# Weights and half of batch 1's x requested right behind batch 0's x; weights loaded row by row with columns picked by TensorE; transposes of x placed in other slots

## The chip, the core and the metric

The kernel runs on one core of a Trainium2 chip. The core has a matrix engine (TensorE, PE in the profile; PEld is its weight load), VectorE (DVE), ScalarE (ACT), GpSimd (POOL) and SyncE (SP), each with its own instruction stream, and sixteen DMA engines that move data between the chip's main memory (HBM), the on-chip memory SBUF and back. The metric is the device time of one execution in microseconds, lower is better.

## The reference

Two attention blocks through 32 inducing points, and behind them a gated feed-forward layer on every token. The shapes are B = 4 batches, N = 12416 tokens, m = 32 inducing points, C = 128 channels, 1536 hidden units.

```python
def mab(q, kv):
    s = scale * (q @ kv.transpose(0, 2, 1))
    s = s - s.max(-1, keepdims=True)
    a = np.exp(s)
    a /= a.sum(-1, keepdims=True) + 1e-09
    return a @ kv
h = mab(I, x)          # I: the inducing points, for each batch
y = mab(x, h)
...
gate = 1.0 / (1.0 + np.exp(-(y @ w_gate)))
val = y @ w_val
out = gate * val @ w_out
```

## The kernel before

The 12416 tokens of a batch lie as 128 partitions by 97 columns of tokens; the columns form six groups of 16 and one group of a single column. Each batch goes through three stages.

Stage 1 (`h`): x is loaded and converted to 16 bits (`x_load`, GpSimd's DMA queue, tile `xn`), turned so that channels lie on partitions (`xT`), scored against the inducing points (`s1_score`), turned into weights by an exponential (`s1_exp`, tile `a1T`), the weights are turned (tile `a1`, named `a` in the profile) and summed with x (`s1_sum`). For batch 0 TensorE turns x and the weights (`x_turn`, `s1_turn_pe`), since everything waits for it. For batches 1 to 3 DMA transposes on SyncE's queue do it (`x_transpose_dma`, L90, and `s1_turn_dma`, L251), beside the work of the batch before. The seven parts are combined (`plan_combine`), and `hw_fill` (L333) multiplies `h` with the gate and value weights, so that stage 3 needs `hw` alone: `hw` is laid out as six columns `i` of two halves `t`, each with 128 hidden units.

Stage 2 (each token's weights over the 32 points): `plan_stage2` scores a group, lowers by the maximum, takes the exponential, divides by the sum on GpSimd and turns the result by a DMA transpose (`s2_turn_dma`, L556, tile `a2r`). For batch 0 the first 4 columns are turned by TensorE, and the next 4 and 8 by the two transposes of L783 and L785.

Stage 3 is the main loop. It goes through blocks of 512 tokens and, within a block, through eight steps with two and one of the twelve hidden groups by turns. A step fills the value half (`hidden_mm`, L810) and, two steps ahead, the gate half, takes a tanh on ScalarE (L828), multiplies both on VectorE (`u`, L839), and TensorE projects `u` with `wo16` (L868). ScalarE scales the result, SyncE stores it (L888). From step 4 on, a product with two groups also waits for the gate fill of two steps later.

Nothing is scheduled by the compiler: each engine executes in the order in which the code is written. Two steps are one slot. The work of stages 1 and 2 is put into slots with `at(slot, ...)`, counted from the first slot `o` of a batch, and comes out between the products of that slot (`beside`). Engines don't wait for a slot, only for the semaphores that their instructions name; so SyncE and GpSimd run ahead of the slot as far as their data lets them. Loads from GpSimd take eight landing semaphores in turn, so the ninth request waits until the first load has landed, and so on.

Before the change the three weights are requested from within batch 0's stage 1 (L671, L674 and L707), the first half of batch 1's x behind the last of them (L716), the other three groups in slots 3, 14 and 17 (L922). The transposes of batch 1's x are in slots 0, 5, 10, 15, 20, 25 and 12 (L919). The last of the batch's seven parts is the single column, seventh in `groups`. Batch 1's first two groups are scored in slots 9 and 13 and summed from slots 16 and 18 on (L908).

Of the kernel before, what the change touches and what calls it, by code (L numbers as in the profile page):

```python
# [10 lines left out]
F16 = mybir.dt.float16  # L11
# [6 lines left out]
P = 128  # L18
# [7 lines left out]
def kernel(  # L26
# [9 lines left out]
    nc = tc.nc  # L36
    B, N, C = x.shape
    m = inducing.shape[0]
    F = moe_w_gate.shape[1]
    NJ = F // P  # L40
    NI = NJ // 2
    NCH = N // P
    NG = NCH // GC
# [8 lines left out]
    const = ctx.enter_context(tc.tile_pool(name="const", bufs=1))  # L52
# [20 lines left out]
    def x_load(b, s, first=0):  # L73
        c0, n = groups[s]
        if s == 0:
            c0, n = 0, n + NLO
        if b not in xn:
            xn[b] = xnp.tile([P, NCH, C], F16, tag="xn", name=f"xn_{b}")
        cuts = [c0, c0 + first, c0 + n] if first else [c0, c0 + n]
        for c, e in zip(cuts, cuts[1:]):  # L80
            nc.gpsimd.dma_start(xn[b][:, c:e, :], xv[b, :, c:e, :])  # L81
# [18 lines left out]
    def keep_on(n, tag):  # L100
        w_ps = ps.tile([P, 4, P], F32, tag=tag, name="w_ps")
        for _ in range(n):
            nc.tensor.matmul(w_ps[:], idle[:, 0, :], idle, start=True, stop=True)
# [18 lines left out]
    )  # L122
    x_load(0, 1)
    x_load(0, 2)
    wg16 = const.tile([P, NI, 2, P], F16, tag="wg16")
    wv16 = const.tile([P, NI, 2, P], F16, tag="wv16")
    wo16 = const.tile([P, NJ, C], F16, tag="wo16")
    x_load(0, 3)
    x_load(0, 4)
    x_load(0, 5, GC - BC)  # L130

    ident = const.tile([P, P], F16, tag="ident")
    nc.vector.tensor_copy(out=ident[:], in_=identf[:])
# [41 lines left out]
    def s1_sum(b, s, a1, tag):  # L175
        hp = ps.tile([P, C + 1], F32, tag=tag, name="hp_ps")
        s1_sum_pe(b, s, a1, hp, 0, 4)
        return s1_sum_keep(b, s, hp)
# [3 lines left out]
    def at(slot, make, late=False):  # L182
        plan.setdefault((slot, late), []).append(make)
# [34 lines left out]
    def s1_score(b, s, tag):  # L218
        s1 = s1_score_pe(b, s, tag)
        s1_max(b, s, s1)  # L220
        return s1
# [107 lines left out]
    def hw_fill(b, hf, tag):  # L329
        hw_ps = ps.tile([P, NI // 2, P], F32, tag=tag, name="hw_ps")  # L330
        for r in range(4):
            wsrc = wg16 if r < 2 else wv16
            nc.tensor.matmul(  # L333
                hw_ps[32 * r : 32 * r + 32, :, :],
                hT16[b][:],
                wsrc[:, ts(hf, NI // 2), r % 2, :],
                start=True,
                stop=True,
            )
        return hw_ps  # L340
# [292 lines left out]
    for p in range(-2, NS - 3):  # L633
        if p + 2 < NS - 1:
            x_turn(0, *groups[arrival[p + 2]], ("g2", "v2")[p % 2])
            if p < 0:
                keep_on((3, 2)[p + 2], "acc")
        if p + 1 >= 0:
            s = arrival[p + 1]
            a1T[s] = s1_exp(0, s, s1_score(0, s, ("g1", "v1")[(p + 1) % 2]))  # L640
        if p >= 0:
            s = arrival[p]
            a1[s] = s1_turn_copy(s, s1_turn_pe(0, s, a1T[s]))
        if p - 1 >= 0:
            s = arrival[p - 1]
            s1_sum(0, s, a1[s], "acc")
        if p + 1 == EARLY - 1:

            we = const.tile([P, EARLY], F32, tag="we")
            nc.vector.tensor_reduce(  # L650
                out=nml[:, 0:1], in_=nm1[:, 0:EARLY], axis=AX.X, op=ALU.min
            )
            nc.scalar.activation(
                out=we[:], in_=nm1[:, 0:EARLY], func=AF.Exp, bias=nml[:, 0:1], scale=-1.0
            )
            lw = const.tile([P, EARLY], F32, tag="lwe")
            nc.gpsimd.tensor_tensor(out=lw[:], in0=l1[:, 0:EARLY], in1=we[:], op=ALU.mult)
            add_tree(lw, EARLY, l1l[:, 0:1])
            hpart = [const.tile([P, C], F32, name=f"hpart{k}", tag=f"hpart{k}") for k in range(2)]

            def pool_part(p):
                nc.gpsimd.tensor_scalar_mul(
                    out=hpart[p > 0][:], in0=hst[:, p, 0:C], scalar1=we[:, p : p + 1]
                )
                if p > 0:
                    nc.gpsimd.tensor_tensor(
                        out=hpart[0][:], in0=hpart[0][:], in1=hpart[1][:], op=ALU.add
                    )

            pool_part(0)  # L670
            nc.gpsimd.dma_start(wg16[:], moe_w_gate.rearrange("c (i t f) -> c i t f", t=2, f=P))  # L671
        elif p == EARLY - 1:
            pool_part(1)
            nc.gpsimd.dma_start(wv16[:], moe_w_val.rearrange("c (i t f) -> c i t f", t=2, f=P))  # L674
        elif p == EARLY:
            pool_part(2)

# [26 lines left out]
    e32s = const.tile([P, m], F32, tag="e32s")  # L704
    nc.scalar.mul(out=e32s[:], in_=e32[:], mul=lsum[:])
    top = join_min(const, ml, (1, 3))
    nc.gpsimd.dma_start(wo16[:], moe_w_out.rearrange("(j p) c -> p j c", p=P))  # L707
    w4 = const.tile([P, 1], F32, tag="w4")
    nc.scalar.activation(out=w4[:], in_=ml[:], func=AF.Exp, bias=top[:], scale=-1.0)
    e32l = const.tile([P, m], F32, tag="e32l0")  # L710
# [2 lines left out]
    )  # L713
    e32w = const.tile([P, m], F32, tag="e32w")
    nc.scalar.mul(out=e32w[:], in_=e32[:], mul=w4[:])
    for g in range(3):  # L716
        x_load(1, g)

    a1[sc] = s1_turn_copy(sc, s1_turn_pe(0, sc, a1T[sc], "v2"))
    hps.append(s1_sum(0, sb, a1[sb], "m"))  # L720
# [173 lines left out]
    for b in range(B):  # L894
        o = base[b]
        more = b + 1 < B

        if b == 0:
            plan_stage2(0, groups[1][0], o, None, o + 3, soon=True)
            plan_stage2(0, groups[2][0], o + 5, o + 7, o + 18)  # L900
        for s in range(3 if b == 0 else 2, NG - 1):
            k = o + 16 * s - 28
            plan_stage2(b, groups[s][0], k, k + 2, k + (14 if more else 10))
        plan_stage2(b, groups[NG - 1][0], o + 56, o + 58, o + 66, far=o + 52)
        if not more:
            continue
        early = (
            [(9, (16, 17, 17)), (13, (18, 19, 19))]  # L908
            if b == 0
            else [(8, (15, 16, 17)), (12, (18, 19, 19))]  # L910
        )
        later = [(24, (31, 31, 31)), (28, (35, 35, 35)), (40, (47, 48, 49)), (44, (50, 51, 51))]
        for s, (score, total) in enumerate(early + later + [(32, (43, 43, 43))]):
            plan_stage1(b + 1, s, o + score, [o + e for e in total])
        plan_combine(b + 1, o + 52, o + 55, [(o + 72, o + 74), (o + 80, o + 82)])
        plan_stage2(b + 1, groups[0][0], o + 67, o + 70, o + 78)
        plan_stage2(b + 1, groups[1][0], o + 84, o + 86, o + 94)
        for g in range(NS):
            when = 3 * g if b else 5 * g if g < NG else 12  # L919
            at(o + when, lambda b=b, g=g: x_transpose_dma(b + 1, g))  # L920
            if b == 0 and 3 <= g < NG:
                at(o + (3, 14, 17)[g - 3], lambda g=g: x_load(1, g))  # L922
        if b + 2 < B:
            for g in range(NG):
                at(o + (24, 33, 42, 60, 60, 82)[g], lambda b=b, g=g: x_load(b + 2, g))

    def beside(slot, late):
        for make in plan.pop((slot, late), ()):
# [53 lines left out]
```

## Time and profile before

| | |
|---|---|
| median of the runs | 732.54 us |
| the three runs | 739.2, 731.61, 732.54 us |
| span of the profiled execution, first to last instruction | 731.7 us |
| mean granted clock of TensorE | 0.992 |
| VectorE busy | 706.5 us (97%) |
| ScalarE busy | 675.3 us (92%) |
| TensorE busy | 650.5 us (89%) |
| GpSimd busy | 420.0 us (57%) |
| moved by DMA | 65.21 MB, 89 GB/s in the mean |

The profile holds one execution; its times are counted from the start of its span. A row of a group gives line, engine, operation, tile written and tiles read, shape and count, then busy time and mean length, then the engine's idle time just before such instructions and what ended most of it. A row of the timeline gives start, length, the instruction, and in brackets the idle time before it with what ended it. The time of a DMA row is that from its issue to its landing. A busy share doesn't say what an engine is worth to the whole; the waits of the engine that is full nearly everywhere do.

### The profile page before, as it was taken

What the parts mean: (1) busy time and instruction counts of PE and PEld (TensorE: products, weight loads), DVE (VectorE), ACT (ScalarE), POOL (GpSimd) and SP (SyncE); (2) the same over time, 40 slices, a digit from 0 to 9 for tenths busy, and PEclk for the clock granted to TensorE, in tenths of its full rate; (3) what the DMA queues carried; (4) which work ended last, traced back from release to release, by engine and by line L of the source; (5) the groups of instructions that cost most, each with busy time, mean ns of one, the idle gap of its engine ahead of it and who ended that gap; (6) DMA issues with size and microseconds to landing.
All of it is one profiled execution on the core that took longest, in us unless ns stands there. A gap on an engine that the chain in (4) does not pass through costs nothing.

```text
span 731.7 us, 21494 instructions
## 1 busy us (share of the span) xinstructions
PE 650.5 (89%) x8437; PEld 391.8 (54%) x8437; DVE 706.5 (97%) x874; ACT 675.3 (92%) x1011; POOL 420.0 (57%) x702
## 2 busy tenths in 40 slices
PE   7978898999988989999988989899999899898887
PEld 3444555655555555555555555555555555555555
DVE  4879899999999999999999999999999999999998
ACT  4669899999999999999999999999999999999996
POOL 3534737588765457398747275487865665646200
PEclk9989999999999999999999999999999999999999
DMA  9899674235358363325188531321222222131311
GB/s 172 138 114 196 122 136 91 56 87 120 64 126 160 75 137 77 81 60 121 44 129 145 118 82 38 88 59 45 75 60 52 61 64 62 42 74 44 60 45 45
DMA packets 117750, 65.21 MB, mean 89 GB/s; under 512 B 101360, under 2 KB 102032, under 8 KB 117648
## 3 DMA queue, kind: packets, MB, share of 16 engines
q1 hardware_dynamic: 111936, 49.81, 31.7%
q0 software_dynamic: 5440, 13.90, 11.4%
q8 instruction: 66, 1.08, 0.6%
q14 instruction: 36, 0.29, 0.1%
q10 hardware_dynamic: 272, 0.13, 0.1%
HBM read 27.80 MB, written 25.43 MB: 73 GB/s over the span
## 4 chain that ended last, share of the span: by engine, by line
DVE 49%; issue 20%; PE 15%; ACT 10%; DMA 4%; DVEq 1%; POOL 0%; ACTq 0%; POOLq 0%
DVE u L839 47%; ACT t L828 9%; PE acc_ps L868 7%; PE v_ps L810 6%; DMA xn<-in_x_dram 2%; DVE nm L214 1%; DMA a2r<-a2n 1%; DMA a<-a1T 1%; DVEq L839 1%; PE hp_ps L262 1%; PE g_ps L810 1%; ACT a1T L227 0%; PE s_ps L202 0%; POOL xn L81 0%; PE xt_ps L624 0%
## 5 line engine op out<-in xcount | busy, mean ns | idle before, releaser
L839 DVE SCALAR_TENSOR_TENSOR u<-t,v_ps 128x1024 f16<-128x1024 f16 (+1 forms) x777 | 675.5, 945 | 8.4 <-PE g_ps L810 4.8
L828 ACT ACTIVATE t<-g_ps 128x1024 f16<-128x1024 f32 (+1 forms) x776 | 593.3, 818 | 36.2 <-ACT t L828 17.0
L810 PE MATMUL v_ps<-a2r,hwt 32*128 32x512 f16 (+1 forms) x1188 | 294.4, 372 | 65.3 <-DVE u L839 64.3
L868 PE MATMUL acc_ps<-wo,u 128*128 128x128 f16 x4656 | 329.4, 221 | 0.0
L868 PEld LDWEIGHTS <-u 128*128 128x128 f16 x4656 | 262.7, 98 | 89.1 <-issue 88.2
L810 PE MATMUL g_ps<-a2r,hwt 32*128 32x512 f16 (+1 forms) x1188 | 297.9, 379 | 2.9 <-DMA a2r<-a2n 2.9
L810 PEld LDWEIGHTS <-hwt 32*128 32x128 f16 x2400 | 90.7, 91 | 200.3 <-issue 152.9
L499 POOL TENSOR_TENSOR sum<-e 128x256 f32<-128x256 f16 (+1 forms) x23 | 15.5, 672 | 149.3 <-ACT e L491 142.7
L545 POOL TENSOR_TENSOR a2n<-e,rs 128x2048 f16<-128x2048 f16 (+2 forms) x24 | 86.2, 3594 | 8.3 <-DVE rs L517 6.6
L523 POOL TENSOR_TENSOR near<-sme,minus 128x16 f32<-128x16 f32 (+1 forms) x22 | 65.2, 2966 | 1.8
L886 ACT ACTIVATE o<-acc_ps 128x512 f32<-128x512 f32 x96 | 58.1, 605 | 0.3 <-PE acc_ps L868 0.3
L478 POOL TENSOR_SCALAR rise<-rise 128x256 f32<-128x256 f32 (+6 forms) x110 | 51.2, 466 | 9.7
L477 POOL TENSOR_TENSOR rise<-sc 128x256 f32<-128x256 f32 (+1 forms) x22 | 16.2, 738 | 38.7 <-ACT sc L467 38.5
L479 POOL TENSOR_TENSOR top<-top,rise 128x128 f32<-128x128 f32 (+3 forms) x88 | 28.4, 323 | 7.3
L499 POOL TENSOR_TENSOR sum<-sum 128x128 f32<-128x128 f32 (+3 forms) x92 | 28.5, 310 | 7.2
L477 POOL TENSOR_TENSOR rise<-top 128x128 f32<-128x128 f32 (+3 forms) x88 | 27.3, 310 | 6.9
L482 POOL TENSOR_TENSOR sc<-sc,top 128x512 f32<-128x512 f32 (+1 forms) x22 | 23.9, 1086 | 1.7
L430 PEld LDWEIGHTS <-xT 128*128 128x128 f16 x388 | 13.1, 96 | 12.0 <-issue 11.9
L430 PE MATMUL s_ps<-hT,xT 128*128 128x32 f16 x388 | 18.1, 178 | 0.1
L479 POOL TENSOR_TENSOR top<-sc,rise 128x256 f32<-128x256 f32 (+1 forms) x22 | 16.2, 738 | 1.8
L227 ACT ACTIVATE a1T<-s_ps,nm 128x512 f16<-128x512 f32 (+1 forms) x24 | 15.1, 629 | 1.7 <-DVE nm L214 1.7
L262 PE MATMUL hp_ps<-xn,a 128*32 128x128 f16 x388 | 14.1, 223 | 2.3 <-DMA a<-a1T 2.0
(121 smaller groups left out, 240.2 us busy)
## 6 DMA issues: line engine op xcount, KB each, us to landing
out_dram<-o SPq DMA_DIRECT2D x96, 256.0 KB, 2.2
xn<-in_x_dram POOLq DMA_DIRECT2D x19, 512.0 KB, 8.0
xn<-in_x_dram POOLq DMA_DIRECT2D x4, 544.0 KB, 5.7
a2r<-a2n SPq DMA_TRANSPOSE x29, 4.5
xn<-in_x_dram POOLq DMA_DIRECT2D x1, 384.0 KB, 15.1
wg<-in_moe_w_gate_dram POOLq DMA_DIRECT2D x1, 384.0 KB, 5.6
wv<-in_moe_w_val_dram POOLq DMA_DIRECT2D x1, 384.0 KB, 6.3
wo<-in_moe_w_out_dram POOLq DMA_DIRECT2D x1, 384.0 KB, 5.8
```

The costliest lines, as they stand in the source:

```text
L430: nc.tensor.matmul(s2[:, j, :], xT[b][:, c + j, :], hT16[b][:], start=(j == 0), stop=whole and j == j1 - 1, skip_group_check=True,)
L477: nc.gpsimd.tensor_tensor(out=r, in0=far, in1=near, op=ALU.subtract)
L478: nc.gpsimd.tensor_scalar_max(out=r, in0=r, scalar1=0.0)
L479: nc.gpsimd.tensor_tensor(out=top[:, 0:n, 0:w], in0=near, in1=r, op=ALU.add)
L499: nc.gpsimd.tensor_tensor(out=d[:, 0:n, :], in0=src[:, :, 0:w], in1=src[:, :, w : 2 * w], op=ALU.add)
L523: nc.gpsimd.tensor_tensor(out=near[:, 0:n], in0=sme[:, 0:n], in1=minus1[:, 0:n], op=ALU.pow)
L545: eng.tensor_tensor(out=a2n[:, 0:n, :, :], in0=e.unsqueeze(2).to_broadcast((P, n, 4, m)), in1=rs.unsqueeze(2).unsqueeze(3).to_broadcast((P ...
L810: st[what + "end"] = nc.tensor.matmul(pt[:, k, col : col + nb * P], hw[b][r : r + 32, j // 2, :], a2r[r : r + 32, o : o + nb, :].rearrange ...
L828: st["tanh"] = nc.scalar.activation(out=st["t"][:], in_=st["g"][:], func=AF.Tanh, scale=0.5)
L839: u = nc.vector.scalar_tensor_tensor(out=st["u"][:, :, c:e], in0=st["t"][:, :, c:e], scalar=1.0, in1=st["v"][:, :, c:e], op0=ALU.add, op1= ...
L868: nc.tensor.matmul(acc[0][(i // 2) % len(acc[0])][:, i, :], st["u"][:, k, ts(i, P)], wo16[:, j, :], start=(j == 0 and i in ((0, 2) if len( ...
L886: nc.scalar.mul(out=o32[:], in_=acc[0][0][:], mul=0.5)
```

## The change

The diff, with the parts left out that only move lines:

```diff
-    wg16 = const.tile([P, NI, 2, P], F16, tag="wg16")
-    wv16 = const.tile([P, NI, 2, P], F16, tag="wv16")
-    wo16 = const.tile([P, NJ, C], F16, tag="wo16")
     x_load(0, 3)
     x_load(0, 4)
     x_load(0, 5, GC - BC)
+    wg16 = const.tile([P, F], F16, tag="wg16")
+    wv16 = const.tile([P, F], F16, tag="wv16")
+    wo16 = const.tile([P, NJ, C], F16, tag="wo16")
+    nc.gpsimd.dma_start(wg16[:], moe_w_gate)
+    nc.gpsimd.dma_start(wv16[:], moe_w_val)
+    nc.gpsimd.dma_start(
+        wo16[:].rearrange("p j c -> p (j c)"), moe_w_out.rearrange("(p j) c -> p (j c)", j=NJ)
+    )
+    for g in range(3):
+        x_load(1, g)
...
-                wsrc[:, ts(hf, NI // 2), r % 2, :],
+                wsrc[:].rearrange("c (f i t) -> c i t f", i=NI, t=2)[:, ts(hf, NI // 2), r % 2, :],
...
-            nc.gpsimd.dma_start(wg16[:], moe_w_gate.rearrange("c (i t f) -> c i t f", t=2, f=P))
...
-            nc.gpsimd.dma_start(wv16[:], moe_w_val.rearrange("c (i t f) -> c i t f", t=2, f=P))
...
-    nc.gpsimd.dma_start(wo16[:], moe_w_out.rearrange("(j p) c -> p j c", p=P))
...
-    for g in range(3):
-        x_load(1, g)
...
-            [(9, (16, 17, 17)), (13, (18, 19, 19))]
+            [(11, (18, 19, 19)), (16, (23, 23, 23))]
             if b == 0
...
-            when = 3 * g if b else 5 * g if g < NG else 12
+            when = 3 * g if b else (7, 10, 13, 16, 19, 22, 11)[g]
             at(o + when, lambda b=b, g=g: x_transpose_dma(b + 1, g))
             if b == 0 and 3 <= g < NG:
-                at(o + (3, 14, 17)[g - 3], lambda g=g: x_load(1, g))
+                at(o + 2, lambda g=g: x_load(1, g))
         if b + 2 < B:
             for g in range(NG):
-                at(o + (24, 33, 42, 60, 60, 82)[g], lambda b=b, g=g: x_load(b + 2, g))
+                at(o + (28 if b == 0 else 24, 33, 42, 60, 60, 82)[g], lambda b=b, g=g: x_load(b + 2, g))
```

The hidden units are numbered anew: unit `f*12 + j` stands where `j*128 + f` stood. `wo` can then be loaded with whole rows, twelve of them to a partition, where it came in pieces of 128 numbers; the gate and value weights lie in SBUF as they lie in HBM, and the fills of `hw` pick every twelfth column.

GpSimd's stream at the program's start, before the change; `xn_92` is batch 0's x, `xn_496` batch 1's, and in brackets stand the semaphores waited for (`DMASW0` to `DMASW7` are landings of loads in turn):

```order
L81 DMA xn_92<-in_x_dram 128x2176
...
L81 DMA xn_92<-in_x_dram 128x512
L137 MEMSET ones_114 128x1
L139 MEMSET ones 128x128
L657 TENSOR_TENSOR lw<-l_0_132,we 128x3 [waits Activation_49]
...
L671 DMA wg_103<-in_moe_w_gate_dram 128x1536
...
L674 DMA wv_104<-in_moe_w_val_dram 128x1536 [waits DMASW0_49]
...
L707 DMA wo_105<-in_moe_w_out_dram 128x12x128 [waits DMASW1_49]
L81 DMA xn_496<-in_x_dram 128x2176 [waits DMASW2_49]
L81 DMA xn_496<-in_x_dram 128x2048 [waits DMASW3_49]
L81 DMA xn_496<-in_x_dram 128x2048 [waits DMASW4_49]
```

The same after it; `xn_113` is batch 1's x:

```order
L81 DMA xn_92<-in_x_dram 128x512
L131 DMA wg_107<-in_moe_w_gate_dram 128x1536
L132 DMA wv_108<-in_moe_w_val_dram 128x1536 [waits DMASW0_49]
L133 DMA wo_109<-in_moe_w_out_dram 128x1536 [waits DMASW1_49]
L81 DMA xn_113<-in_x_dram 128x2176 [waits DMASW2_49]
L81 DMA xn_113<-in_x_dram 128x2048 [waits DMASW3_49]
L81 DMA xn_113<-in_x_dram 128x2048 [waits DMASW4_49]
L144 MEMSET ones_121 128x1
L146 MEMSET ones 128x128
L664 TENSOR_TENSOR lw<-l_0_139,we 128x3 [waits Activation_49]
```

The six requests moved ahead of GpSimd's own first sums. The last of them waits for the landing of the fifth load of batch 0's x (`DMASW4`), and what follows it in the stream waits with it.

SyncE's stream from the first transposes of stage 2 to the second turned weights of batch 1, before; `xT_676` is the turned x of batch 1, `a_1089` and `a_1225` are its turned stage-1 weights:

```order
L556 DMA_TRANSPOSE a2r<-a2n 128x8x128 [waits Pool_49]
L90 DMA_TRANSPOSE xT_676<-xn_496 128x16x128 [waits DMASW2_49]
L888 DMA out_dram<-o_838 128x512 [waits Activation_49]
L90 DMA_TRANSPOSE xT_676<-xn_496 128x16x128 [waits DMASW3_49]
L556 DMA_TRANSPOSE a2r<-a2n 128x16x128 [waits Pool_49]
L888 DMA out_dram<-o_1006 128x512 [waits Activation_49]
L90 DMA_TRANSPOSE xT_676<-xn_496 128x16x128 [waits DMAHW0_49,DMASW4_49]
L251 DMA_TRANSPOSE a_1089<-a1T 128x4x128 [waits DMAHW1_49,PE_49,Activation_49]
L90 DMA_TRANSPOSE xT_676<-xn_496 128x1x128 [waits DMAHW2_49]
L888 DMA out_dram<-o_1142 128x512 [waits DMAHW3_49,Activation_49]
L251 DMA_TRANSPOSE a_1225<-a1T 128x4x128 [waits DMAHW4_49,PE_49,Activation_49]
```

And after; `xT_933`, `a_1154` and `a_1338` are the same three:

```order
L563 DMA_TRANSPOSE a2r<-a2n 128x8x128 [waits Pool_49]
L890 DMA out_dram<-o_838 128x512 [waits Activation_49]
L90 DMA_TRANSPOSE xT_933<-xn_113 128x16x128 [waits DMASW2_49]
L563 DMA_TRANSPOSE a2r<-a2n 128x16x128 [waits Pool_49]
L890 DMA out_dram<-o_1007 128x512 [waits Activation_49]
L90 DMA_TRANSPOSE xT_933<-xn_113 128x16x128 [waits DMASW3_49]
L90 DMA_TRANSPOSE xT_933<-xn_113 128x1x128 [waits DMAHW0_49]
L890 DMA out_dram<-o_1141 128x512 [waits DMAHW1_49,Activation_49]
L258 DMA_TRANSPOSE a_1154<-a1T 128x4x128 [waits DMAHW2_49,PE_49]
L90 DMA_TRANSPOSE xT_933<-xn_113 128x16x128 [waits DMAHW3_49,DMASW4_49]
L90 DMA_TRANSPOSE xT_933<-xn_113 128x16x128 [waits DMAHW4_49,DMASW5_49]
L890 DMA out_dram<-o_1275 128x512 [waits DMAHW5_49,Activation_49]
```

The first transpose of x moved behind the store of block 0, the second behind that of block 1, and the first turned weights of batch 1 behind that of block 2.

## The prediction

> **What bounds the kernel now.** I read the page's head and its costliest groups first, then busy time by stretches, then VectorE's timeline, then the chain of waits and the transfers. The groups show that the product of the two hidden halves on VectorE (L839) is the main load, and that its waiting for others is 8.4 us in all.
>
> ```profile
> span 731.7 us, 21494 instructions
> L839 DVE SCALAR_TENSOR_TENSOR u<-t,v_ps 128x1024 f16<-128x1024 f16 (+1 forms) x777 | 675.5, 945 | 8.4 <-PE g_ps L810 4.8
> ```
>
> The stretches (columns: window, length, busy time of PE, weight loads, VectorE, ScalarE, GpSimd, granted clock, DMA share, GB/s) say where. VectorE is full from 80 to 100 us, where only less VectorE work could help. It is not full from 37 to 46 us and from 60 to 80 us, where the granted clock falls too.
>
> ```profile
> 37.00:42.00 5.00, 1.71 (x19) 1.02 (x19) 2.04 (x3) 1.41 (x2) 0.82 (x2) 0.87 1.23 136
> 42.00:46.00 4.00, 4.00 (x25) 1.64 (x21) 2.13 (x3) 2.31 (x4) 1.29 (x3) 0.50 1.37 127
> 60.00:80.00 20.00, 16.85 (x247) 10.04 (x244) 16.93 (x21) 16.43 (x27) 7.83 (x17) 0.91 1.07 193
> 80.00:100.00 20.00, 17.47 (x246) 10.54 (x242) 20.00 (x25) 19.24 (x30) 13.78 (x23) 1.00 0.63 126
> ```
>
> VectorE's timeline (start, length, instruction, idle time before it) has the first product at 33.13 us and names six waits in two clusters: 3.42 + 1.41 + 0.38 = 5.21 us, and 1.45 + 0.62 + 1.00 = 3.07 us. Their 8.28 us are all but 0.1 of the 8.4, so nothing else is to be had there.
>
> ```profile
> 33.13 2.99 DVE L839 SCALAR_TENSOR_TENSOR u<-t,v_ps 128x1024 f16<-128x1024 f16 x3
> ...
> 42.46 1.82 DVE L839 SCALAR_TENSOR_TENSOR u<-t,v_ps 128x1024 f16<-128x1024 f16 x2 [3.42 <-PE v_ps L810]
> 45.69 1.82 DVE L839 SCALAR_TENSOR_TENSOR u<-t,v_ps 128x1024 f16<-128x1024 f16 x2 [1.41 <-PE g_ps L810]
> 47.88 2.95 DVE L839 SCALAR_TENSOR_TENSOR u<-t,v_ps 128x1024 f16<-128x1024 f16 x3 [0.38 <-PE g_ps L810]
> ...
> 74.32 0.69 DVE L839 SCALAR_TENSOR_TENSOR u<-t,v_ps 128x512 f16<-128x512 f16 x1 [1.45 <-PE g_ps L810]
> 75.63 1.82 DVE L839 SCALAR_TENSOR_TENSOR u<-t,v_ps 128x1024 f16<-128x1024 f16 x2 [0.62 <-PE g_ps L810]
> 78.45 8.13 DVE L839 SCALAR_TENSOR_TENSOR u<-t,v_ps 128x1024 f16<-128x1024 f16 x9 [1.00 <-PE g_ps L810]
> ```
>
> TensorE, which runs in order, was itself held by a transfer at the head of each cluster: by the turned weights of the second block (`a2r`), and by the turned stage-1 weights of batch 1 (`a`).
>
> ```profile
> 41.81 0.60 PE L810 MATMUL g_ps<-a2r,hwt 32*128 32x512 f16 x2 [2.92 <-DMA a2r<-a2n]
> 73.58 0.24 PE L262 MATMUL hp_ps<-xn,a 128*32 128x128 f16 x4 [1.97 <-DMA a<-a1T]
> ```
>
> The chain of waits agrees (start, length, what): the first part is set by a load of batch 0's x that landed at 18.0 us, and the transpose asked for at 33.18 us took 8.59.
>
> ```profile
> 4.00 14.04 DMA xn<-in_x_dram
> 33.18 8.59 DMA a2r<-a2n
> ```
>
> **The first cluster.** In the page's list of issues (the last number is the median time to landing) a transpose of 128x512 and one of 128x2048 take 2.6 and 4.5 us. What stood in the way of the one at 33.18 us were three loads of x, asked for from 26.94 us on; behind them here are the DMA rows of the first and the third, issued at 26.94 and 28.00 us.
>
> ```profile
> a<-a1T SPq DMA_TRANSPOSE x18, 2.6
> xT<-xn SPq DMA_TRANSPOSE x21, 4.5
> ```
> ```profile
> 26.94 1.62 POOL L81 DMA_DIRECT2D xn<-in_x_dram  x3
> ```
> ```profile
> xn<-in_x_dram POOLq DMA_DIRECT2D x1, 544.0 KB, 7.7
> xn<-in_x_dram POOLq DMA_DIRECT2D x1, 512.0 KB, 11.8
> ```
>
> The first landed at 34.6 us, the third at 39.8: 2.6 us for each 512 KB. The transpose landed 41.8 - 39.8 = 2.0 us after the last load, so it comes through once the loads are gone. After the change the three weights and these loads stand in GpSimd's queue right behind batch 0's x, of which 512 KB are still out at 18.0 us; it is in at 20.6. At 2.6 us per 512 KB, three weights of 384 KB take 5.9 us and 544 + 512 + 512 KB 8.0 us: the last load lands at 34.5 us, 5.3 us sooner, and the transpose at 36.5 us. TensorE began to wait at 41.81 - 2.92 = 38.9 us. With 2.4 us to spare the wait goes, and so do the two short ones behind it, which belong to the halved clock (0.50) after the idle time: 5.21 us. What is late next is the turned x, below.
>
> GpSimd pays with waits: each of the later requests waits for the landing of an earlier load, the last for the one that landed at 18.0 us. Behind it in GpSimd's order stand the sums of batch 0's first stage, which ran at 15.44 us.
>
> ```profile
> 15.44 0.19 POOL L657 TENSOR_TENSOR lw<-l,we 128x3 f32<-128x3 f32 x1 [9.58 <-ACT we L653]
> 21.69 0.60 POOL L662 TENSOR_SCALAR hpart<-hst,we 128x128 f32<-128x128 f32 x1 [2.29 <-ACT hst L277]
> ```
>
> From 15.44 to 21.69 us they spend 2.29 us on their last wait, so they have some slack, and two weight requests no longer stand among them. Starting at 19.0 us instead they need some 2.5 us and are at the piece of 21.69 us in time. I cost this at nothing; 1 us if x lands a microsecond later. The weights are in at 20.6 + 5.9 = 26.5 us, ahead of their first use at 28.39 us (below). That they come row by row, `wo` above all, saves packets beside work that waits for none of them: nothing.
>
> **The second cluster.** `a` was asked for at 66.53 us and reached TensorE at 73.58, 7.0 us instead of 2.6, beside two loads that GpSimd issued from 63.22 us on.
>
> ```profile
> 63.22 1.17 POOL L81 DMA_DIRECT2D xn<-in_x_dram  x2
> 66.53 1.31 SPq L251 DMA_TRANSPOSE a<-a1T  x1
> ```
>
> These loads move to slot 2, next to the one at 37.28 us. No load of x then stands before slot 28, and the stage-1 sum is planned five slots after its transpose instead of three; a slot, two products, is 8.13 / 9 x 2 = 1.8 us. So these 3.07 us go as well. TensorE and VectorE execute the same instructions, in other slots.
>
> **The weights' columns.** The fills of `hw` read their moving operand with a step of twelve elements instead of one. No row has such a step. The nearest are the same fills now, and a matmul whose moving operand has step zero:
>
> ```profile
> 28.39 0.34 PE L333 MATMUL hw_ps<-wg,hT 128*32 128x384 f16 x2
> ...
> 28.57 0.33 PE L333 MATMUL hw_ps<-wg,hT 128*32 128x384 f16 x2
> ...
> 29.67 0.32 PE L454 MATMUL s_ps<-hi,identb 128*128 128x384 bf16 x1 [0.23 <-POOL hi L445]
> ```
>
> 0.32 us against 0.33: the step need not cost anything, and a gain has no reason. If reading ran at a quarter, the two fills, 0.18 us apart, would add 3 x 2 x 0.18 = 1.1 us; the wait of 0.23 us at 29.67 takes up a part, so some 0.8 us would reach the start of the products. I take 0, nearest to the row of step zero. [...]
>
> **The turned x.** SyncE's transposes of batch 1's x now stand behind the store of block 0, issued at 48.11 us; 5.2 us sooner that is 42.9, and the first starts near 43.3. By then three loads are on their way (from 37.28 us; a lone load takes 5.2 us, two more 2.6 each: until 47.7 us). What a transpose costs beside a load differs. The first of these rows is the store; the DMA answers below it are, in order, of the transpose at 37.04, of the load at 37.28, of the load at 194.25, of the transpose at 195.28 and of a lone load at 161.5 us.
>
> ```profile
> 48.11 0.38 SPq L888 DMA_DIRECT2D out_dram<-o  x1
> ```
> ```profile
> 37.04 5.46 SPq L90 DMA_TRANSPOSE xT<-xn  x1
> ...
> 37.28 0.60 POOL L81 DMA_DIRECT2D xn<-in_x_dram  x1
> ```
> ```profile
> 194.25 0.65 POOL L81 DMA_DIRECT2D xn<-in_x_dram  x1
> ```
> ```profile
> 195.28 6.80 SPq L556 DMA_TRANSPOSE a2r<-a2n  x1
> ```
> ```profile
> xT<-xn SPq DMA_TRANSPOSE x1, 17.9
> ```
> ```profile
> xn<-in_x_dram POOLq DMA_DIRECT2D x1, 512.0 KB, 16.9
> ```
> ```profile
> xn<-in_x_dram POOLq DMA_DIRECT2D x1, 512.0 KB, 8.0
> ```
> ```profile
> a2r<-a2n SPq DMA_TRANSPOSE x1, 10.3
> ```
> ```profile
> xn<-in_x_dram POOLq DMA_DIRECT2D x1, 512.0 KB, 5.2
> ```
> ```profile
> 55.02 0.40 PE L202 MATMUL s_ps<-xT,indT 128*32 128x512 f16 x4 [0.17 <-DMA xT<-xn]
> ```
>
> A transpose asked for 0.24 us ahead of a load took 17.9 us; one asked for 1.0 us behind a load took 10.3, landing 3.3 us after that load, which took 8.0 instead of 5.2. Here the loads are six us ahead, nearest to the second pair: 47.7 + 3.3 = 51.0 us, or 53.8 if the loads stretch by 2.8 us as that one did. The scores (last row) need it two slots later than now: 55.0 - 5.2 + 3.6 = 53.4 us. That is a wait of 0 to 0.4 us, and up to 1.7 with the store's 256 KB in front (half of 2.6 us). I take 0.5. Behind it on SyncE stands the `a2r` of the second group: after an issue of 6.8 us as at 195.28 it starts at 50.1 us and lands 4.5 us later, while slot 15, which fills from it, is at 33.1 + 15 x 1.8 = 60.1 us.
>
> [...]
>
> **The sum.** 731.7 - 5.2 - 3.1 + 0.5 = 723.9 us of span. The runs shown are 731.61, 732.54 and 739.2 us, so the span is within 0.1 us of the lowest and 0.8 below the median; I add 0.4: 724.3 us.
>
> **The rivals.** *The turned x is late by some us*: the stretch (53.8) and the whole of the store (2.6) make it 56.4 us, 3.0 us of waiting, and a halved clock behind it another 1.41 + 0.38: 4.8 us, 731.7 - 8.3 + 4.8 + 0.4 = 728.6 us. For it speak the 7.0 us of `a`, against it the loads' lead. 0.20. *The loads still lie before the first transposes*, because GpSimd's waits let the queue run dry and the lead isn't had: only 3.1 us are gained, 729.0 us; it decides where the last load lands after 38.9 - 2.0 = 36.9 us. 0.07. [...] 0.09. *Slower*: transposes and loads throttle each other from the first turned x on, as at 37.04 us. At 43.3 us some 1.7 of the three loads are out; at 16.9 us each they need 28.7 us, x is turned 3.3 us later, at 75.3 us, and the wait is 21.9 + 1.8 us: 747.5 us. With 17.9 us for the transpose it is 61.2 us and 733.4. From a landing at 59.9 us on it eats the gain. For it stands that one pair of rows, against it the pair of 194 us. 0.09.
>
> **How the numbers follow.** The forecast holds 0.55, at 723.3 to 725.5 us. The range 722.8 to 729.5 takes in the two rivals near 729 and the slow reads; it leaves out the slower one and what is below the sum. One per cent, about what a measurement of this kernel can tell from no change, is 7.3 us: 725.2 and 739.9 us. Faster: most of the forecast (0.47) and half of the slow reads, 0.52. Slower: 0.06, the worse part of the last rival. Within: 0.42.
>
> **What would show it.** L839 with under 1.5 us of waiting; VectorE full in 37 to 46 and 60 to 80 us, with the clock at 1.00; the third load of batch 1 landed by 36.9 us; the first turned x before 53.4 us; the fill still at 0.33 us; the first product still at 33.1 us. The forecast is wrong if the products start over 0.5 us later, or if a new wait for `xT` or `a` stands before 80 us.

## The result and the profile after

The changed kernel takes 728.14 us (median of six runs, 727.66 to 728.62); the kernel before, beside it, 735.64 us (six runs, 731.61 to 739.2). The ratio is 0.9895, 95% interval 0.9855 to 0.9935: faster by 1.05%. The forecast was 724.3 us in a range of 722.8 to 729.5. The profiled execution took 727.66 us, of which 725.8 is its span.

The page and the groups of the kernel after (L841 is the product that was L839; lines behind the new loads have moved by two):

```profile
span 725.8 us, 21496 instructions
L841 DVE SCALAR_TENSOR_TENSOR u<-t,v_ps 128x1024 f16<-128x1024 f16 (+1 forms) x777 | 675.6, 944 | 3.1 <-PE g_ps L812 2.9
```

The product's waiting has gone from 8.4 to 3.1 us. The stretches (same columns as before: window, length, busy PE, weight loads, VectorE, ScalarE, GpSimd, clock, DMA share, GB/s) show VectorE nearly full where it was not, and a clock of 1.00 in place of 0.87, 0.50 and 0.91:

```profile
37.00:42.00 5.00, 4.46 (x61) 2.84 (x59) 4.70 (x7) 4.33 (x7) 2.75 (x7) 1.00 0.98 169
42.00:46.00 4.00, 3.69 (x55) 2.21 (x51) 4.00 (x7) 3.69 (x6) 1.44 (x4) 1.00 1.06 183
60.00:80.00 20.00, 17.51 (x277) 10.77 (x273) 19.53 (x24) 19.05 (x30) 10.92 (x13) 1.00 0.81 140
80.00:100.00 20.00, 17.98 (x278) 11.03 (x277) 19.98 (x26) 19.13 (x31) 8.61 (x21) 1.00 0.68 134
```

VectorE's timeline has two small waits where the clusters were, and two more, which the kernel before did not have, soon after batch 1 begins. Four like these stand at 336.89, 351.21, 508.31 and 522.62 us, the same places in batches 2 and 3.

```profile
32.26 1.82 DVE L841 SCALAR_TENSOR_TENSOR u<-t,v_ps 128x1024 f16<-128x1024 f16 x2
...
40.21 4.68 DVE L841 SCALAR_TENSOR_TENSOR u<-t,v_ps 128x1024 f16<-128x1024 f16 x5 [0.30 <-PE g_ps L812]
...
77.05 1.22 DVE L841 SCALAR_TENSOR_TENSOR u<-t,v_ps 128x1024 f16<-128x1024 f16 x1 [0.36 <-PE g_ps L812]
...
165.48 13.95 DVE L841 SCALAR_TENSOR_TENSOR u<-t,v_ps 128x1024 f16<-128x1024 f16 x16 [0.36 <-PE g_ps L812]
179.79 2.95 DVE L841 SCALAR_TENSOR_TENSOR u<-t,v_ps 128x1024 f16<-128x1024 f16 x3 [0.36 <-PE g_ps L812]
```

The rows of the fills of `hw` (L340, once L333) say what came in their place. One took 0.33 us before; the first of them in the timeline, and the group of all 16 for the gate weights (busy us, mean ns), now read:

```profile
27.53 0.86 PE L340 MATMUL hw_ps<-wg,hT 128*32 128x384 f16 x2
```
```profile
L340 PE MATMUL hw_ps<-wg,hT 128*32 128x384 f16 x16 | 6.5, 836 | 0.0
```

The transfers did what was asked of them. On GpSimd the last load of batch 1's first half is issued at 17.03 us, and the sums behind it run at 17.75 and 20.39 us:

```profile
17.03 0.53 POOL L81 DMA_DIRECT2D xn<-in_x_dram  x1 [1.93 <-DMA xn<-in_x_dram]
...
17.75 0.21 POOL L664 TENSOR_TENSOR lw<-l,we 128x3 f32<-128x3 f32 x1
...
20.39 0.60 POOL L669 TENSOR_SCALAR hpart<-hst,we 128x128 f32<-128x128 f32 x1 [0.16 <-POOL hpart L673]
```

In the lists of DMA issues (the last number is the time to landing) that load takes 16.1 us, so it lands at 33.1 us. The first transpose of `a2r`, asked for at 32.32 us, takes 2.6 instead of 8.6. The first turned x, issued on SyncE at 42.66 us, takes 9.0 and is there at 51.7 us.

```profile
xn<-in_x_dram POOLq DMA_DIRECT2D x1, 512.0 KB, 16.1
```
```profile
a2r<-a2n SPq DMA_TRANSPOSE x1, 2.6
```
```profile
xT<-xn SPq DMA_TRANSPOSE x1, 9.0
```

The books: 731.7 - 8.28 (both clusters) + 0.30 + 0.36 + 6 x 0.36 - 0.87 (the first product at 32.26 instead of 33.13 us) = 725.4 us, against 725.8 measured.

### The profile page after: what moved, and what is told of

It is laid out like the page before. It is cut to its first block, busy times and chain, and to the rows that moved or that the text cites. A ratio compares the mean times of both kernels' runs of the same rounds, so it can differ in the third digit from the quotient of the medians.

```text
span 725.8 us, 21496 instructions
## 1 busy us (share of the span) xinstructions
PE 648.4 (89%) x8437; PEld 390.4 (54%) x8437; DVE 706.7 (97%) x874; ACT 676.7 (93%) x1011; POOL 419.4 (58%) x702
## 4 chain that ended last, share of the span: by engine, by line
DVE 50%; issue 21%; PE 17%; ACT 9%; DMA 2%; DVEq 1%; POOL 0%; ACTq 0%; POOLq 0%
DVE u L841 47%; ACT t L830 8%; PE acc_ps L870 8%; PE v_ps L812 6%; DMA xn<-in_x_dram 2%; DVE nm L221 2%; PE hw_ps L340 1%; DVEq L841 1%; ACT a1T L234 1%; PE g_ps L812 0%; PE hp_ps L269 0%; POOL xn L81 0%; ACT hwt L419 0%; PE w_ps L103 0%; PE s_ps L437 0%
## 5 line engine op out<-in xcount | busy, mean ns | idle before, releaser
L841 DVE SCALAR_TENSOR_TENSOR u<-t,v_ps 128x1024 f16<-128x1024 f16 (+1 forms) x777 | 675.6, 944 | 3.1 <-PE g_ps L812 2.9
L81 POOL DMA_DIRECT2D xn<-in_x_dram x25 | 14.7, 596 | 6.6 <-DMA xn<-in_x_dram 5.7
```

The costliest lines, as they stand in the source:

```text
L841: u = nc.vector.scalar_tensor_tensor(out=st["u"][:, :, c:e], in0=st["t"][:, :, c:e], scalar=1.0, in1=st["v"][:, :, c:e], op0=ALU.add, op1= ...
```

## The experiments

Spans are compared, which lie 1.7 to 1.9 us under the times. The shortest of all are 722.9 to 723.1 us. All kernels but e2 number the hidden units as the kernel before does, if nothing else is said.

**The two halves of the change.** `e3_loads_early` has the early loads and batch 0's old slots; `e4_slots_only` has the kernel before's loads and the new slots.

```
e3:  the weights and x_load(1, 0..2) asked for behind batch 0's x, wo in its old pieces
     scores at (9, ..), (13, ..); x turned at 5 * g and 12; x_load(1, 3..5) at 3, 14, 17; x_load(2, 0) at 24
e4:  the reverse: loads where the kernel before has them,
     scores at (11, ..), (16, ..); x turned at 7, 10, 13, 16, 19, 22, 11; x_load(1, 3..5) at 2; x_load(2, 0) at 28
```

> The loads of the weights and of half of batch 1's x behind the first x, with the old numbering of the hidden units and every slot of batch 0 as before the change. My theory, that the first cluster is the three x loads running beside the first transpose and the second cluster is the load of batch 2's x beside a transpose, so that each falls to its own part of the change: the first cluster (3.42 + 1.41 + 0.38 = 5.2 us at 42 to 48 us) goes, the second (3.1 us at 74 to 79 us) stays; span 731.7 - 5.2 = 726.5 us, and 725.6 if the 0.9 us at the start come with the early loads too. Rival, the early loads do everything: span 722.5-723.7 us with no wait of the product over 1.5 us. Second rival, the old slots of x_load(1, 3..5) and of the turned x meet with the first transposes all the same: the first cluster stays at over 3 us and the span is 729-732 us.

> The kernel before with the moved slots alone (the scores of the first batch's next selection two to five steps later, the turned x, the loads of batch 1's second half and of batch 2's first block moved); weights and batch 1's first half are asked for where they were. My theory: the first cluster stays at 4 to 5.2 us or shifts by the two steps, at least half of it, because the three loads still land after 36.9 us beside the first transpose; the second goes; span 731.7 - 3.1 = 728.6 us, down to 726.5 if the later scores wait less. Rival, the later scores alone give the transposes the time that they need: both clusters go, span 723.4-724.5 us. Second rival, the loads of batch 1's second half, now asked for together, meet the first transposes: over 6 us of waits before 55 us and a span over 731 us.

Measured: e3 735.66 us median, ratio 0.9967 (0.9916 to 1.0017), its spans from 726.3 to 737.6 us, the longest that of the profiled execution; e4 729.42 us, ratio 0.9883 (0.9822 to 0.9944), spans 726.8 to 729.0 us. VectorE's timeline of e4 keeps the first cluster and has nothing of the second but one wait of 0.36 us:

```profile
41.15 1.82 DVE L839 SCALAR_TENSOR_TENSOR u<-t,v_ps 128x1024 f16<-128x1024 f16 x2 [2.65 <-PE v_ps L810]
43.55 1.82 DVE L839 SCALAR_TENSOR_TENSOR u<-t,v_ps 128x1024 f16<-128x1024 f16 x2 [0.59 <-PE g_ps L810]
45.72 2.95 DVE L839 SCALAR_TENSOR_TENSOR u<-t,v_ps 128x1024 f16<-128x1024 f16 x3 [0.35 <-PE g_ps L810]
```

e3 has the opposite. Its profiled execution is one of its longer ones, so only the order of events is read from it. VectorE is full where the first cluster stood; from 60 to 80 us it waits, at a clock of 0.70, behind a transpose of `a` that was asked for at 61.35 us beside two loads of x and took 7.2 us:

```profile
42.00:46.00 4.00, 3.75 (x56) 2.38 (x56) 4.00 (x7) 3.90 (x6) 1.27 (x6) 1.00 1.00 184
46.00:50.00 4.00, 3.49 (x46) 1.97 (x41) 4.00 (x6) 3.80 (x7) 4.00 (x2) 1.00 0.67 122
...
60.00:80.00 20.00, 17.65 (x226) 10.73 (x224) 13.85 (x17) 13.66 (x22) 8.36 (x11) 0.70 0.84 139
```

Behind it stands, in this execution, a third stall of which the profile before has nothing: 5.07 us and, right behind, 1.20 and 0.69. There a transpose of `a` asked for at 91.27 us, beside two loads issued from 90.64 us on, took 10.8 us.

```profile
103.47 0.69 DVE L839 SCALAR_TENSOR_TENSOR u<-t,v_ps 128x512 f16<-128x512 f16 x1 [5.07 <-PE g_ps L810]
```

So in these profiles each cluster belongs to its own half, as the theory had it, but e3 as a whole missed the expected 726.5 us: the early loads alone can't be told from no change, and which of the old slots makes the third stall, and whether the shorter runs have it, is open. What the theory had wrong is that a cluster has one size. The first is 5.2 us before and 3.6 in e4. e2 (further down), with loads and slots at their old places, has 1.27 + 1.41 us there, then 1.63 + 1.20 + 0.54 from 54 us on, where the scores wait for the turned x, and 2.93 + 1.20 + 0.85 in the second cluster. The slots are therefore worth more than 3.1 us: e4's ratio is 8.6 us of some 735. They also take away spread: over 7 us in the runs of the kernel before, 2.2 us in e4, 1.0 in the changed kernel.

**Which of the moved slots.** Each of these undoes one of the moves in `e1_old_columns` (further down), whose spans are 723.0 to 723.7 us, with one of 725.4.

```
e9:   at(o + 2, ...)                           ->  at(o + (3, 14, 17)[g - 3], ...)     x_load(1, 3..5)
e10:  (7, 10, 13, 16, 19, 22, 11)[g]           ->  5 * g if g < NG else 12            the turned x
e8:   [(11, (18, 19, 19)), (16, (23, 23, 23))] ->  [(9, (16, 17, 17)), (13, (18, 19, 19))]
e7:   28 if b == 0 else 24                     ->  24                                 x_load(2, 0)
```

> As e1_old_columns, but the second half of batch 1's x is asked for at slots 3, 14 and 17 again instead of all at slot 2. Theory, that the second cluster and the long spans come from loads of x that meet a transpose of a or of x at 58 to 72 us, and that the halved clock behind each stall makes them longer: new waits of the product between 60 and 80 us, 3 us or more in the profiled run, with the granted clock under 1.00 there; spans spread over 3 us or more, from 724 us up, median 2 to 10 us above that of e1_old_columns. Rival, the later scores of the first batch's end (slots 11 and 16) already give the transposes time: no wait over 0.5 us after 50 us and a median within 1 us of e1_old_columns (724-726 us).

> As e1_old_columns, but batch 1's x is turned at slots 0, 5, 10, 15, 20, 25 and 12 again, so that the first transpose is asked for within 1.5 us of the three loads of x at slot 2. The rival of the prediction that ends slower, transposes and loads throttling each other from the first on: the first transpose takes 15 us or more instead of 9, the loads 10 to 17 us each, a2r of the second group comes late behind it on SyncE, TensorE stalls over 2 us before 60 us, and the span is 726-733 us. Theory of this run, that the transpose's slack covers it since the scores come at slot 11: the transpose and the loads take long, but no wait of the product over 0.5 us, span 722.5-724.5 us.

> As e1_old_columns, but the scores of batch 1's first two blocks stand at slots 9 and 13 again and their sums at 16, 17 and 18, 19, while the transposes of x and the loads stay where the change put them. Theory, that the later scores are needed because the first turned x lands at 51.7 us now: at slot 9 the scores want it at 33 + 9 x 1.8 = 49.5 us, so TensorE waits 1.5 to 3 us there, the clock halves behind it, and the span is 725-728 us. Rival, the scores have slack: no wait over 0.5 us, span 722.5-723.7 us.

> As e1_old_columns, but the first load of batch 2's x stands at slot 24 again instead of 28. Theory, that this move is the smallest part: the load is asked for some 7 us sooner, at 77 to 83 us, where the transposes of batch 1 are still under way; no wait over 0.5 us, span within 0.5 us of e1_old_columns (722.5-724.2 us). Rival, as in the run with the early loads alone, where loads at 90.6 us met a transpose of a asked for at 91.3 us and TensorE waited 5 us: a stall of 2 us or more between 75 and 105 us with the clock at 0.5 behind it, span 726 us or more in at least half of the runs.

Measured, medians and ratios: e9 728.29 us, 0.9895 (0.986 to 0.9931); e10 724.91, 0.9858 (0.9795 to 0.992); e8 729.41, 0.9909 (0.9879 to 0.9939); e7 725.17, 0.9855 (0.9794 to 0.9916). Spans: e9 724.0 to 728.8, e10 722.9 to 725.3, e8 725.8 to 729.3, e7 722.9 to 724.1.

In e9 a part of the second cluster is back, with its cause. The profiled execution is one of its two best, with 0.73 + 0.36 us of waits at a clock of 1.00, less than the 3 us expected; the other eight runs are 2 to 4.8 us longer, with mean clocks of 0.991 to 0.998, and no trace shows where they lose it. The transpose of `a`, asked for at 57.47 us, took 9.6 us beside two loads issued from 57.24 us on, where the changed kernel's took 4.0, and TensorE waited for it:

```profile
67.11 0.24 PE L267 MATMUL hp_ps<-xn,a 128*32 128x128 f16 x4 [1.26 <-DMA a<-a1T]
```
```profile
67.86 0.69 DVE L839 SCALAR_TENSOR_TENSOR u<-t,v_ps 128x512 f16<-128x512 f16 x1 [0.73 <-PE g_ps L810]
68.91 8.86 DVE L839 SCALAR_TENSOR_TENSOR u<-t,v_ps 128x1024 f16<-128x1024 f16 x10 [0.36 <-PE g_ps L810]
```
```profile
a<-a1T SPq DMA_TRANSPOSE x1, 9.6
```

In e10 the meeting that the prediction's slower rival was made of does take place: a turned x asked for at 35.32 us, 1.1 us ahead of three loads, takes 15.1 us. It does no harm: it is there at 50.4 us, sooner than the changed kernel's 51.7, and with the scores at slot 11 nothing needs it before 52.30 us.

```profile
35.32 10.50 SPq L90 DMA_TRANSPOSE xT<-xn  x1
```
```profile
xT<-xn SPq DMA_TRANSPOSE x1, 15.1
```

In e8 the scores want the turned x before it lands at 52.2 us: TensorE stands still from 49.8 us on, VectorE waits 1.87 us, and 1.20 + 0.54 more once TensorE has begun again. The stretches show the clock at 0.50 from 52 to 58 us:

```profile
52.26 0.62 PE L207 MATMUL s_ps<-xT,indT 128*32 128x512 f16 x4 [2.48 <-DMA xT<-xn]
```
```profile
52.92 0.69 DVE L219 TENSOR_REDUCE nm<-s_ps 128x1 f32<-128x512 f32 x1 [1.87 <-PE s_ps L207]
55.41 1.82 DVE L839 SCALAR_TENSOR_TENSOR u<-t,v_ps 128x1024 f16<-128x1024 f16 x2 [1.20 <-PE g_ps L810]
57.77 4.67 DVE L839 SCALAR_TENSOR_TENSOR u<-t,v_ps 128x1024 f16<-128x1024 f16 x5 [0.54 <-PE g_ps L810]
```
```profile
51.00:52.00 1.00, 0.00 (x0) 0.00 (x0) 0.05 (x1) 0.12 (x1) 0.92 (x2) 0.83 1.28 113
52.00:53.00 1.00, 0.74 (x6) 0.21 (x5) 0.08 (x1) 0.00 (x0) 0.83 (x3) 0.50 1.25 284
...
57.00:58.00 1.00, 1.00 (x8) 0.22 (x6) 0.46 (x2) 0.72 (x2) 0.92 (x2) 0.50 0.01 1
58.00:59.00 1.00, 1.00 (x14) 0.86 (x12) 1.00 (x2) 1.00 (x2) 0.18 (x1) 0.75 0.21 43
```

So two moves work, the loads at slot 2 and the later scores; the turned x and batch 2's first load could have stayed where they were. Whether the later scores are still needed with the transposes back at their old slots was not run.

**What the halved clock costs by itself.** `e11_keep_busy` is e8 with work for TensorE during its wait.

```
+        if b == 1 and s == 0:
+            for k in range(11):
+                nc.tensor.matmul(s1[0:32, :], indT[:], wo16[:, 0:4, :]..., start=True, stop=True)
```

> As e8_scores_back, where TensorE stands still from 49.8 to 52.3 us for the turned x, the clock then is 0.5 from 51.2 to 58.5 us, and VectorE waits 1.87 + 1.20 + 0.54 us; here 11 matmuls of 128x512 whose result nobody uses (the scores overwrite it) are put on TensorE ahead of that wait, 11 x 0.22 = 2.4 us at full clock. Theory, that the two later waits are the price of the halved clock and not of the stall itself: the clock stays at 1.00 from 50 to 60 us in the profile, the first wait stays at 1.5 to 2.2 us, the two behind it shrink to under 0.5 us together, the span is 725.5-726.0 us, and the median lies 1 to 3 us under the 729.4 us of e8_scores_back. Rival, they come from TensorE having lost its lead over VectorE: the clock stays at 1.00 or nearly, but over 1.2 us of waits still follow the first, span 727 us or more. Second rival, matmuls that use 32 columns of the array don't keep the clock up: it halves all the same and nothing changes, or the fillers cost 2 us more.

Measured: 729.17 us median (727.64 to 731.79), span of the profiled execution 726.1 against 727.2 in e8. In the profile the clock stays at 1.00 and the two waits behind the first are gone, though the turned x came 0.7 us later (53.0 us) and the first wait is longer:

```profile
53.45 0.69 DVE L224 TENSOR_REDUCE nm<-s_ps 128x1 f32<-128x512 f32 x1 [2.41 <-PE s_ps L212]
```
```profile
50.00:60.00 10.00, 8.69 (x87) 4.75 (x85) 7.45 (x9) 6.73 (x11) 6.91 (x16) 1.00 0.97 171
```

In these two profiles that tells the halved clock from the lost lead: the later waits were the clock's, 1.7 us of them. The medians do not differ as expected. Four of e11's ten runs have a mean clock of 1.000 and spans of 725.8 to 726.4 us, none of e8's ten has; in the other six it is 0.992 to 0.998, so there it fell all the same, and no trace shows where.

**The columns.** `e1_old_columns` is the changed kernel with contiguous columns, `e2_new_columns` the kernel before with the new ones; `e5_step2` and `e6_step6` number the units so that TensorE reads every second or sixth element, 4 or 12 bytes from one to the next.

```
e1:  wsrc[:].rearrange("c (i t f) -> c i t f", i=NI, t=2)      wo16 <- "(j p) c -> p j c"
e2:  the kernel before with wg16, wv16 as [P, F], wo "(p j) c -> p (j c)" and "c (f i t) -> c i t f"
e5:  "c (i f t) -> c i t f"                                    wo in 6 pieces of 2 rows
e6:  "c (h f i t) -> c h i t f", h=2                           wo in 2 pieces of 6 rows
```

> The changed kernel with the hidden units numbered as before: the weights are still asked for behind the first x and every slot stays moved, but TensorE reads 128 contiguous elements of a weight row instead of every twelfth. My theory, that the six waits of 0.36 us at the fills of batches 1 to 3 and the fill at 831 ns come from the reads 24 bytes apart: the fill falls back to 326 to 337 ns, the six waits (6 x 0.36 = 2.2 us) go, the eight fills at the start take 0.5 us instead of 1.5, and the span falls from 725.8 to 722.5-723.7 us. Rival, the moved slots make these waits: the fill is short again, but the waits of the product at 165 to 523 us stay, and the span is 724.8-725.8 us. Second rival, the output weights in 128 x 12 pieces of 256 bytes take the software queue longer than one block: batch 1's first x lands more than 2 us later than at 28.8 us, and 1 to 3 us come back before 50 us.

> The kernel before with the new numbering of the hidden units alone: the weights are loaded row by row at their old places, the columns picked by TensorE 24 bytes apart, no slot moved. My theory: the fill goes from 335 to 831 ns, six new waits of about 0.36 us appear at the fills of batches 1 to 3, the first product comes 0.5 to 1 us later, both clusters of waits (5.2 us at 42 to 48 us, 3.1 us at 74 to 79 us) stay; span 731.7 + 2.2 + 0.5 to 1.0 = 734.4-734.9 us, which is slower than the kernel before. Rival, the fills hide behind TensorE's idle time and the small waits belong to the moved slots: no such waits, span 731.7-732.5 us. Second rival, loading in whole rows is what removed the clusters: the span falls below 730 us.

> As e1_old_columns, but the units are numbered so that TensorE reads every second element of a weight row: 4 bytes from one to the next, four of them in 16 bytes. [...] Rival, any step but one costs: fill at 500 to 831 ns and six waits of about 0.36 us.

> [...] Rival, by elements as soon as they lie some bytes apart: 831 ns and six waits of 0.36 us. [...]

Measured: e1 725.21 us, ratio 0.983 (0.9769 to 0.9891), spans 723.0 to 723.7 us in three of four runs; e2 735.42 us, 0.9961 (0.9918 to 1.0004); one run each of e5 and e6, with spans of 723.1 and 725.7 us (in e6 the first product comes 0.8 us later than in e5, for a reason that isn't the reads', see below). The groups of the fill in e1, e2, e5 and e6, in that order:

```profile
L338 PE MATMUL hw_ps<-wg,hT 128*32 128x384 f16 x16 | 2.5, 335 | 0.0
```
```profile
L333 PE MATMUL hw_ps<-wg,hT 128*32 128x384 f16 x16 | 6.6, 840 | 0.0
```
```profile
L338 PE MATMUL hw_ps<-wg,hT 128*32 128x384 f16 x16 | 2.6, 341 | 0.0
```
```profile
L338 PE MATMUL hw_ps<-wg,hT 128*32 128x384 f16 x16 | 5.2, 668 | 0.0
```

The stretch from 140 to 700 us holds nothing else that differs, and VectorE's third number in it is the price. First e1, then the changed kernel, e2 and e6:

```profile
140.00:700.00 560.00, 505.34 (x6507) 305.18 (x6506) 559.97 (x662) 538.81 (x794) 343.32 (x558) 1.00 0.37 81
```
```profile
140.00:700.00 560.00, 505.19 (x6472) 304.23 (x6471) 557.78 (x658) 537.40 (x791) 341.85 (x557) 1.00 0.36 80
```
```profile
140.00:700.00 560.00, 505.62 (x6482) 304.72 (x6479) 557.77 (x660) 537.12 (x793) 350.49 (x573) 1.00 0.36 80
```
```profile
140.00:700.00 560.00, 505.58 (x6486) 304.99 (x6485) 558.67 (x659) 537.78 (x792) 342.79 (x558) 1.00 0.36 80
```

559.97 - 557.78 = 2.2 us, six waits of 0.36, with the new slots and with the old ones: the reads make these waits, not the slots. At 12 bytes it is 559.97 - 558.67 = 1.3 us, in six waits of 0.20 to 0.23; at 4 bytes nothing (559.97 again). The rivals of the two runs, 500 to 831 ns at 4 bytes and 831 at 12, did not come true with 341 and 668. The two small waits of 0.30 and 0.36 us at 40 and 77 us stand in e1 and e5 too, so they are not the reads'. The first is in every profile with the early loads; the second is in every one with the later scores, e4 among them, and not in e8 and e11, which have the scores back. That e2 would be slower than the kernel before was not seen: both vary by more than 2 us in their clusters. Nor did the output weights in small pieces delay batch 1's x: in e1 its first load lands at 28.6 us, against 28.8 in the changed kernel.

**The parts that are needed, alone.** `e12_needed_only` is e1 with the moves of e10 and e7 undone together.

> The parts that the runs so far show to be needed, and no other: the early loads with the old numbering of the hidden units, the second half of batch 1's x at slot 2, the later scores; batch 1's turned x and batch 2's first load stand where they stood before the change. Theory, that the moved turns and the moved load of batch 2 bring nothing: span 722.5-724.2 us in all runs but those in which the fifth load of x lands at 18 us (725.4 us), median 724.5-725.5 us, ratio to the kernel before 0.980 to 0.988. Rival, the two moves guard against a meeting of loads and transposes that the single undoings did not show because the other was still in place: spans over 726 us in a third of the runs or more.

Measured: 724.88 us median (724.84 to 725.71, six runs), ratio 0.9866 (0.9821 to 0.9911), spans 723.0 to 723.8 us. In these runs the two moves guard against nothing. Its median is 3.3 us under the changed kernel's; by the ratios to the kernel before beside each it is 2.1 us.

## Why the prediction came out as it did

The forecast was the likeliest case and the right one: both clusters went, for the causes it named. It was 3.8 us too low: 3.7 from two terms, the columns and what lies around the span, less 0.7 from three smaller ones, and 0.8 between the sum of these (at the end of this section) and the median.

**First cluster, 5.2 us: right.** The third load landed at 33.1 us (forecast 34.5, deciding point 36.9), the transpose took 2.6 us, and e4, which has the loads late, keeps 2.65 + 0.59 + 0.35 us, so this size too is that of one execution. The view that the short waits belong to the halved clock is what e11 shows for another stall.

**Second cluster, 3.1 us: right cause, one sample.** The loads at slot 2 take it away, and e9, without them, waits 1.26 us for `a` again. But 3.07 us is what it cost in one execution; the kernel before loses other amounts in others, and the mean clock roughly goes with them: 728.9 us of span at 0.995, 733.9 at 0.990, 739.7 at 0.986 among the runs that stood beside the first four experiments. A forecast against the profiled time is sound, one against a median of three such runs is not.

**The turned x, 0.5 us: nothing, in time by 0.7 us.** It landed at 51.7 us, in the forecast's 51.0 to 53.8; the scores began at 52.33 us instead of 53.4, in the main because this execution ran 0.9 us ahead (see below). It took 9.0 us, twice the median of 4.5 us in the profile before; others took 15.1 us (e10) and 17.9 (before), and what makes those so long stays open. The cover named, scores two slots later, is real: without it e8 loses 1.87 + 1.20 + 0.54 = 3.6 us, between the 1.7 us of the main case and the 4.8 us of the rival "late by some us".

**GpSimd's waits at nothing: right.** The sums ran at 17.75 us (forecast 19.0), the piece of 21.69 us at 20.39.

**The columns at 0: wrong, and this is the step that failed.** "I take 0, nearest to the row of step zero": step zero reads one element again and again and says nothing of a read that goes on to another address each time. Measured, the fill took 836 ns at 24 bytes from one element to the next, 668 at 12, 341 at 4 and 335 at 2. No run had shown such a read when the slow reads got their chance of 0.09, and the quarter of the rate behind their 0.8 us is shown by none since: 836 for 335 ns is 2.5 times. They were also priced at the wrong place. At the start, where the 0.8 us were to fall, the fills do take 1.0 us longer (27.53 to 29.06 us, against 28.39 to 28.90 before), but nothing of it reaches the products: the first product stands at 32.26 us, and at 32.24 in e10 with contiguous columns. In later batches no idle time of TensorE covers the fills: two slots in each batch hold a fill, TensorE does not get half a microsecond back there, and 6 x 0.36 = 2.2 us reach the end.

**From span to time, 0.4 us: 1.9.** Every run lists 1.7 to 1.9 us between them. The profiled execution of before, 731.7 us of span, was thus one of about 733.6 us, 1.0 above the median shown; its span was set beside times when it was found within 0.1 us of the lowest run. The term was 1.5 us too small.

**The first product at 33.1 us: 32.26, not forecast and not the change's.** A load of batch 0's x, the fifth, landed at 16.75 us in the profile after, 18.03 before. The chain of waits of the kernel after now starts from the load behind it:

```profile
4.52 14.70 DMA xn<-in_x_dram
```

In the profiles of the experiments the fifth load lands either at 16.6 to 17.0 us (e2, e4, e5, e7, e9, e10, e12) or at 17.9 to 18.2 (e1, e3, e6, e8, e11), and the early side holds kernels with late weights (e2, e4) as well as with early ones (e12). With the early landing the first product comes at 32.24 to 32.58 us, with the late one at 33.03 to 33.22, and in e1's profile, where TensorE's clock then falls, 2.4 us later than in e10's. What decides it stays open. Of the changed kernel's six runs three have spans of 725.8 or 725.9 us and three of 726.8, which is a step of this size, though only the profiled run, one of the short ones, has a trace. So the 0.9 us count as luck of that execution, not as a gain of the change.

Together: 724.3 + 2.2 (columns) + 0.7 (two small waits) + 1.5 (around the span) - 0.5 (turned x) - 0.9 (start) = 727.3 us; the profiled execution took 727.66.

## What to carry to other kernels

A stall of TensorE is priced with the halved clock behind it (1.7 us of waits behind the first one of 1.87 in e8), and by its cause, not by its size in one profile: a transfer that sometimes meets another makes a spread, and the gain of moving it is the spread's mean. A new access pattern with no row in the trace is priced by a run that has it alone, as e2 has the columns (840 ns for 335), at every place where the instruction stands, and the slack that is to cover it is read off the timeline at that place. Of a change with several moves each is worth undoing alone: here two of the four moved slots did the work, and one part, the new columns, took back 2.2 us.

## What the runs showed of the hardware that was not expected

The 128x384 fill took 335 ns at steps of 2 bytes, 341 at 4, 668 at 12 and 836 at 24. So 4 bytes cost 2% more than 2, 12 bytes twice as much, and 24 bytes 2.5 times. What sets the time at each step was not shown.

Up to 715 us of these profiles the clock was at 0.50 for 3.4 us or twice, three or four times as long. Worked out from the stretches of 1 us: 51.66 to 58.5 us in e8 (0.83 and 0.75 at its edges), so 6.8 us; 19.74 to 23.14 us in e1, so 3.4 us. Stretches of other lengths give 6.8 and 3.4 us in the kernel before, 3.4, 6.8 and 6.8 in e2, 13.7 and 10.2 in e3, and 3.4 in e4; the other profiled executions have a mean clock of 0.999 or 1.000. The two falls of one execution lie 34.1 us apart before (40.70 and 74.83 us), ten times 3.41, and 30.7 us in e3 (68.11 and 98.83 us), nine times. What the clock follows was not shown. The length of a gap alone does not decide: TensorE's idle 1.97 us before 18.27 us in e1 are followed by a fall, its 2.07 us before 18.11 us in e8 are not. In e1 the clock fell 1.5 us after TensorE had begun to work again, and in e8 after 1.9 us of standing still, in a gap of 2.48 us:

```profile
19.00:20.00 1.00, 1.00 (x14) 0.51 (x11) 0.63 (x2) 0.63 (x1) 0.84 (x7) 0.87 1.15 226
20.00:21.00 1.00, 1.00 (x23) 0.77 (x22) 0.99 (x3) 0.62 (x2) 1.00 (x2) 0.50 1.07 209
...
23.00:24.00 1.00, 1.00 (x26) 0.58 (x24) 0.83 (x2) 0.27 (x1) 0.01 (x1) 0.93 1.80 183
```
